# Attention times V with V stationary in four column tiles, the sums of E as one more row, outputs repacked and normalized through DRAM scratch

## The chip, the cores and the metric

One core of a Trainium2 chip runs the whole program. The metric is the device time of one execution in microseconds (us). Several executions are taken of each kernel, and the kernel before is run again on the same chip beside every kernel that is compared with it. A ratio is the mean time of one kernel's fast runs over the mean of the other's fast runs of the same rounds, so it is not quite the ratio of the medians quoted here. For a single core, a run is called slow if it lies over 1.5% above the fastest of its kernel.

Engine names in the profile: PE is TensorE's matmul, PEld its weight load, DVE is VectorE, ACT is ScalarE, POOL is GpSimd, SP is the engine that issues DMAs. "Tile" below means 128 rows (tokens) of the sequence, "block" two tiles.

## The reference

Two rounds of a sliding-window attention layer and an MLP, on 2048 tokens of width 512, with 32 heads of 16:

```python
def _A_ref(x, wqkv, wo):
    H = 32; Dh = D // H; W = 256
    q, k, v = ...                                 # x @ wqkv, split into heads
    scores = einsum("bhqd,bhkd->bhqk", q, k) * Dh ** -0.5
    mask = (i - j >= 0) & (i - j < W)
    p = softmax(where(mask, scores, -1e9))
    o = einsum("bhqk,bhkd->bhqd", p, v)
    return merge_heads(o) @ wo
def _B_ref(x, w1, b1, w2, b2):                    # F = 1792
    return gelu(x @ w1 + b1) @ w2 + b2
x = x + _A_ref(_layernorm(x), ...); x = x + _B_ref(_layernorm(x), ...)     # twice
```

The window is two tiles wide, so a tile of queries needs the keys of three tiles. The kernels skip the maximum in the softmax, compute E = exp(scores) with keys on partitions and queries along the free dimension, and divide by the sum at the end.

## The kernel before

The kernel is written as a list of nodes, each with an engine, a duration in ns and a priority. A planner simulates the engines with these durations, picks for each engine the ready node of lowest priority number, and the order that comes out is fixed: on the chip every engine executes its list strictly in order and waits on semaphores.

```python
class _Plan:
    LAT = {"pe": 230.0, "act": 110.0, "dve": 110.0, "pool": 150.0, "sp": 100.0}
    def add(self, eng, fn, dur, reads=(), writes=(), prio=0.0, ...): ...
    def run(self):
        ...                                       # cut: list scheduling in planned time
                if e == "sp":
                    efree[e] = t + 60.0           # an issue of a DMA holds the queue 60 ns
                else:
                    efree[e] = end
        return order
```

PV of one tile and one parity of heads takes E as the stationary operand: for each of four heads and three key tiles a 128x128 piece of E is loaded and 17 columns of V move (16 of the head, one of ones, which gives the sum). The result has tokens on partitions, so 1/sum is one number per partition and head, and O has to be transposed afterwards for the output projection.

```python
def pvm(e, B):
    for r in range(RG):                           # RG = 4 heads
        h = c * HC + 2 * r + par
        for k in range(kmin, t + 1):              # up to 3 key tiles
            x = e.matmul(ps[:, B[g][0], r * VW : (r + 1) * VW],            # VW = 17
                E[:, eslot(tau - t + k, v), r, blk * P : (blk + 1) * P],   # stationary
                Va[:, (tau - t + k) % VR, h, :], start=(k == kmin), stop=(k == t))
add("pe", pvm, ...)
add("dve", reciprocal(R[:, rs, :], <column 16 of each head>), 120, ...)
add("dve", tensor_tensor(out=Otm[...], in0=<O in PSUM>, in1=R[...], op=ALU.mult), ...)
...
def outproj(tau, prio):
    # four transposes of Otm, one copy to OT, then four matmuls with Wo
def mlp(J, ...):                                  # one MLP job for every four tiles
```

The layernorm's last step, `xn = (X - mean) * rstd`, is a VectorE `tensor_scalar`, planned at 330 ns.

The softmax here doesn't subtract the row's maximum and nothing guards it: scores larger than these inputs give would overflow.

## Time and profile before

| | before |
|---|---|
| median of 3 runs | 695.31 us (692.96 to 698.25) |
| TensorE busy | 581.8 us (84%) |
| ScalarE / VectorE / GpSimd busy | 65% / 61% / 31% |
| mean granted TensorE clock | 0.906 |
| first exponential starts | 50.3 us |

The profile page of the kernel before, its first lines and the chain of work that ended last (the path of waits followed back from the end):

```profile
span 694.4 us, 14552 instructions
PE 581.8 (84%) x5984; PEld 298.2 (43%) x5984; DVE 423.9 (61%) x1249; ACT 451.9 (65%) x640; POOL 217.4 (31%) x381
...
PE 56%; DVE 27%; ACT 9%; issue 5%; POOL 2%; POOLq 0%; DVEq 0%
PE ps L504 44%; DVE E L600 6%; PE ps L625 5%; ACT E L593 5%; PE ps L582 5%; DVE KT L540 5%; DVE X L513 4%; ACT E L596 3%; DVE stat L470 3%; DVE xn L480 2%; DVE Va L553 2%; DVE Otm L639 2%; PE ps L488 2%; DVE R L636 1%; DVE QT L532 1%
```

TensorE leads the chain; L504 is the helper that issues all projection and MLP matmuls, L625 is PV. No DMA stands in the chain. The groups of instructions by line that the change touches (busy us, mean ns of one, then idle time of the engine before them):

```profile
L625 PE MATMUL ps<-Va,E 128*128 128x17 bf16 x2880 | 112.4, 173 | 32.1 <-DVE Otm L639 7.7
L639 DVE TENSOR_TENSOR Otm<-ps,R 128x64 bf16<-128x64 f32 x256 | 56.3, 220 | 5.6
L636 DVE RECIPROCAL R<-ps 128x4 f32<-128x4 f32 x256 | 44.6, 174 | 14.6 <-PE ps L625 13.6
```

The timeline of TensorE shows a score group of four row tiles and a PV group of twelve matmuls (start us, length us). Twelve PV matmuls take 0.46 us, 38 ns each:

```profile
606.07 0.34 PE L582 MATMUL ps<-QT,KT 32*128 32x384 bf16 x4 [0.52 <-ACT E L593]
606.35 0.46 PE L625 MATMUL ps<-Va,E 128*128 128x17 bf16 x12
```

Busy time by stretches of the middle (length, then busy us and instructions of PE, PEld, DVE, ACT, POOL; granted clock; DMA share; GB/s):

```profile
300.00:400.00 100.00, 89.08 (x858) 45.68 (x856) 61.39 (x184) 69.54 (x109) 23.05 (x41) 0.91 0.01 1
400.00:500.00 100.00, 90.72 (x925) 45.57 (x925) 65.14 (x186) 69.47 (x95) 35.84 (x58) 0.93 0.01 4
```

In the middle TensorE is busy 90% of the time, and the DMA engines do next to nothing (share 0.01).

### The profile page before, as it was taken

What the parts mean: (1) busy time and instruction counts of PE and PEld (TensorE: products, weight loads), DVE (VectorE), ACT (ScalarE), POOL (GpSimd) and SP (SyncE); (2) the same over time, 40 slices, a digit from 0 to 9 for tenths busy, and PEclk for the clock granted to TensorE, in tenths of its full rate; (3) what the DMA queues carried; (4) which work ended last, traced back from release to release, by engine and by line L of the source; (5) the groups of instructions that cost most, each with busy time, mean ns of one, the idle gap of its engine ahead of it and who ended that gap; (6) DMA issues with size and microseconds to landing.
All of it is one profiled execution on the core that took longest, in us unless ns stands there. A gap on an engine that the chain in (4) does not pass through costs nothing.

```text
span 694.4 us, 14552 instructions
## 1 busy us (share of the span) xinstructions
PE 581.8 (84%) x5984; PEld 298.2 (43%) x5984; DVE 423.9 (61%) x1249; ACT 451.9 (65%) x640; POOL 217.4 (31%) x381
## 2 busy tenths in 40 slices
PE   0277888898889898899978898898989898799878
PEld 0143445444444444544444444444344444344433
DVE  0399788837683767838485677837486574625511
ACT  0008798788388836786187955779488964877340
POOL 2235455315341424400152243414243232410000
PEclk9998687999999888997989999899999998688989
DMA  9400000000000000000000000000000000000000
GB/s 312 142 1 1 1 3 1 2 1 1 1 2 2 2 1 1 2 1 1 1 1 2 1 1 1 2 2 2 23 9 2 1 8 24 1 2 9 24 1 30
DMA packets 10740, 10.89 MB, mean 16 GB/s; under 512 B 2226, under 2 KB 10163, under 8 KB 10675
## 3 DMA queue, kind: packets, MB, share of 16 engines
q1 hardware_dynamic: 10674, 9.97, 4.4%
q8 instruction: 47, 0.77, 0.5%
q14 instruction: 19, 0.15, 0.1%
HBM read 7.87 MB, written 2.10 MB: 14 GB/s over the span
## 4 chain that ended last, share of the span: by engine, by line
PE 56%; DVE 27%; ACT 9%; issue 5%; POOL 2%; POOLq 0%; DVEq 0%
PE ps L504 44%; DVE E L600 6%; PE ps L625 5%; ACT E L593 5%; PE ps L582 5%; DVE KT L540 5%; DVE X L513 4%; ACT E L596 3%; DVE stat L470 3%; DVE xn L480 2%; DVE Va L553 2%; DVE Otm L639 2%; PE ps L488 2%; DVE R L636 1%; DVE QT L532 1%
## 5 line engine op out<-in xcount | busy, mean ns | idle before, releaser
L593 ACT ACTIVATE E<-ps 128x768 bf16<-128x768 f32 (+2 forms) x256 | 198.8, 777 | 197.0 <-PE ps L582 195.2
L605 POOL TENSOR_SCALAR_AFFINE_SELECT E<-E 128x512 bf16<-128x512 bf16 x224 | 161.6, 722 | 264.2 <-ACT E L596 263.8
L596 ACT ACTIVATE E<-ps 128x768 bf16<-128x768 f32 (+2 forms) x256 | 199.0, 777 | 0.0
L625 PE MATMUL ps<-Va,E 128*128 128x17 bf16 x2880 | 112.4, 173 | 32.1 <-DVE Otm L639 7.7
L600 DVE TENSOR_TENSOR E<-E,mask 128x512 bf16<-128x512 bf16 x256 | 123.4, 484 | 20.6 <-ACT E L596 19.7
L625 PEld LDWEIGHTS ps<-Va,E 128*128 128x128 bf16 x2880 | 95.0, 98 | 86.5 <-issue 30.3
L504 PE MATMUL ps<-W_sb,gT 128*128 128x512 bf16 x448 | 113.8, 396 | 0.0
L582 PE MATMUL ps<-QT,KT 32*128 32x384 bf16 (+2 forms) x1024 | 92.3, 350 | 20.3 <-ACT E L593 19.1
L504 PE MATMUL ps<-xnTB,W_sb 128*128 128x512 bf16 x448 | 104.2, 388 | 0.5 <-DVE xnTB L493 0.5
L513 DVE TENSOR_TENSOR X<-X,ps 128x512 bf16<-128x512 bf16 x64 | 44.0, 687 | 91.4 <-PE ps L504 91.1
L684 ACT ACTIVATE gT<-ps,b1T 128x512 bf16<-128x512 f32 x112 | 76.4, 687 | 28.4 <-PE ps L504 28.0
L504 PE MATMUL ps<-xnTA,Wqkv_sb 128*128 128x256 bf16 x512 | 84.3, 311 | 7.4 <-DVE KT L540 4.9
L474 POOL TENSOR_SCALAR veps<-statmv 128x1 f32<-128x1 f32 x64 | 14.9, 233 | 174.4 <-DVE statmv L472 174.0
L504 PEld LDWEIGHTS ps<-xnTB,W_sb 128*128 128x128 bf16 x448 | 42.9, 99 | 50.0 <-issue 3.5
L488 PE MATMUL ps<-ident,xn 128*128 128x128 bf16 x256 | 27.7, 239 | 43.4 <-DVE xn L480 37.4
L504 PEld LDWEIGHTS ps<-W_sb,gT 128*128 128x128 bf16 x448 | 40.9, 100 | 53.4 <-issue 15.4
L504 PEld LDWEIGHTS ps<-xnTA,Wqkv_sb 128*128 128x128 bf16 x512 | 49.2, 108 | 26.7 <-DVE KT L540 7.1
L639 DVE TENSOR_TENSOR Otm<-ps,R 128x64 bf16<-128x64 f32 x256 | 56.3, 220 | 5.6
L663 DVE COPY OT<-ps 128x512 bf16<-128x512 bf16 x32 | 13.4, 419 | 73.9 <-PE ps L658 73.3
L582 PEld LDWEIGHTS ps<-QT,KT 32*128 32x128 bf16 x1024 | 26.3, 93 | 74.4 <-ACT E L593 46.7
L636 DVE RECIPROCAL R<-ps 128x4 f32<-128x4 f32 x256 | 44.6, 174 | 14.6 <-PE ps L625 13.6
L540 DVE TENSOR_SCALAR KT<-ps,parmask 128x512 bf16<-128x512 f32 x64 | 46.3, 738 | 4.4 <-PE ps L504 4.1
(34 smaller groups left out, 374.7 us busy)
## 6 DMA issues: line engine op xcount, KB each, us to landing
W_sb<-in_B_w_dram SPq DMA_DIRECT2D x2, 1792.0 KB, 14.7
out_dram<-X SPq DMA_DIRECT2D x16, 128.0 KB, 1.7
Wqkv_sb<-in_A_wqkv_dram SPq DMA_DIRECT2D x3, 512.0 KB, 5.6
X<-in_A_x_dram SPq DMA_DIRECT2D x1, 1024.0 KB, 11.0
X<-in_A_x_dram SPq DMA_DIRECT2D x2, 256.0 KB, 3.5
X<-in_A_x_dram SPq DMA_DIRECT2D x1, 512.0 KB, 7.9
Wo_sb<-in_A_wo_dram SPq DMA_DIRECT2D x1, 512.0 KB, 8.6
b1raw<-in_B_b_dram SPq DMA_DIRECT2D x1, 3.5 KB, 15.5
```

What stands on the lines that cost most here:

```text
L504: r = e.matmul(ps[:, B[g][0], cols], lhsT, rhs, start=st, stop=sp)
L513: add("dve", lambda e, B: e.tensor_tensor(out=X[:, t, :], in0=X[:, t, :], in1=ps[:, B[g][0], :], op=ALU.add), d_psum(512), reads=["X%d" % ...
L540: kn = (add("dve", lambda e, B, g=g, i=i, par=par: e.tensor_scalar(out=KT[:, kb, par, 2 * i : 2 * i + 2, :], in0=ps[:, B[g][0], :].rearran ...
L582: x = e.matmul(ps[:, bk[r], 0:N], KT[rows, kb, par, c, kc0 : kc0 + P], QT[rows, c, t * P : t * P + N], start=True, stop=True)
L593: a = add("act", lambda e, B, gT3=gT3, es=es: e.activation(E[:, es, 0:2, 0:N], ps[:, B[gT3][0] : B[gT3][0] + 2, 0:N], AF.Exp, scale=SCALE) ...
L596: a2 = add("act", lambda e, B, gS1=gS1, es=es: e.activation(E[:, es, 2:4, 0:N], ps[:, B[gS1][0] : B[gS1][0] + 2, 0:N], AF.Exp, scale=SCALE ...
L600: add("dve", lambda e, B, es=es: e.tensor_tensor(out=E[:, es, :, 0:P], in0=E[:, es, :, 0:P], in1=mask01[:, None, :].to_broadcast([P, RG, P ...
L605: add("pool", lambda e, B, es=es: e.affine_select(E[:, es, :, 2 * P : 3 * P], E[:, es, :, 2 * P : 3 * P], [[0, RG], [-1, P]], ALU.is_ge, 0 ...
L625: x = e.matmul(ps[:, B[g][0], r * VW : (r + 1) * VW], E[:, eslot(tau - t + k, v), r, blk * P : (blk + 1) * P], Va[:, (tau - t + k) % VR, h ...
L636: add("dve", lambda e, B: e.reciprocal(R[:, rs, :], ps[:, B[g][0], 0 : RG * VW].rearrange("p (b d) -> p b d", d=VW)[:, :, Dh]), 120, reads ...
L639: add("dve", lambda e, B: e.tensor_tensor(out=Otm[:, s, c * P : (c + 1) * P].rearrange("p (r a d) -> p r a d", a=2, d=Dh)[:, :, par, :], i ...
L684: gelu_last[0] = add("act", lambda e, B, g=g, fc=fc: e.activation(gT[:, fc, :], ps[:, B[g][0], :], AF.Gelu_apprx_tanh, bias=b1T[:, fc : fc ...
```

## The change

The intent: let TensorE spend less on PV. V (17 columns) becomes the stationary operand, and E, which is wide, moves. Four heads go to four column tiles of the array, so their outputs lie 32 partitions apart in one PSUM bank, with the sum of E as row 16 of each. O arrives transposed, which saves the transposes, but its rows lie in the wrong partitions and the sums lie on other partitions than O. So the bank is copied to SBUF (`OD`), written to DRAM scratch, read back repacked (`On`); the sums are read as 64 rows (`Dc`), inverted, written out again and read back broadcast over 16 partitions (`Rn`); GpSimd multiplies.

```diff
+ for pi, (k, q_lo, q_hi) in enumerate(parts):          # k in (-1, 0, -2, 1)
+     for r in range(RG):
+         x = e.matmul(ps[32 * r : 32 * r + VW, B[g][0], par * 256 + q_lo * P : par * 256 + (q_hi + 1) * P],
+                      Va[:, (2 * b + k) % VR, h, :],                            # stationary, 17 columns
+                      E[:, es, r, (q_lo - k) * P : (q_hi + 1 - k) * P], ...)    # moving, 128 or 256
+ evac(OD[:, s] <- ps)                                    # VectorE, or ScalarE if idle
+ dma(scr[bs, c].rearrange("j r n -> r j n") <- OD[:, s].rearrange("p a q -> p (a q)"))   # scr: (2, 4, 32, 4, 512)
+ dma(On[:, c, :] <- scr[bs, c, 0:Dh].rearrange("j r (a q) -> (j r a) q", a=2))
  ...                                                     # once per block of two tiles:
+ dma(Dc[:, bs, :] <- scr[bs, :, Dh].rearrange("c r (k n) -> c (r k) n", n=P))
+ add("dve", reciprocal(Rc[:, bs, :], Dc[:, bs, :]), 960, ...)
+ dma(scr_r[bs] <- Rc[:, bs, :])
+ for c in range(DC):
+     dma(Rn[:, c, :] <- scr_r[bs, c] broadcast to 16 partitions)
+     add("pool", tensor_tensor(OT[:, bs, c, :], On[:, c, :], Rn[:, c, :], mult), 500, ...)
```

Much else moves with it. The planner may now place some work on either of two engines, its formulas for matmuls, VectorE and ScalarE are changed a little, and all DMAs of the chain are planned at 2.0 us:

```diff
- def dma(fn, writes, reads=(), dur=3000.0, prio=0.0):
+ def dma(fn, writes, reads=(), dur=2000.0, prio=0.0):
      add("dve", tensor_scalar(out=xn[:, s, :], in0=X[:, t, :], ...), 330, ...
+         alt=(("pool", tensor_scalar(out=xn[:, s, :], in0=X[:, t, :], ...), 700, POOL_H),))
+ # masks of E: VectorE or GpSimd; OD copies: VectorE or ScalarE
+ JOBS = [(0, 2), (2, 2), (4, 4), (8, 4), (12, 4), (16, 4), (20, 4), (24, 4), (28, 2), (30, 2)]
- qkv(0, -40)
- qkv(1, -30)
+ lnq(0, -60); kv(0, -50); lnq(1, -40)                    # K and V of block 1 later
  ...                                                     # cut: visits go by blocks, K in one VectorE pass
```

## The prediction

> **What bounds the kernel now.** The page: TensorE busy 84% (582 of 694 us), ScalarE 65%, VectorE 61%, GpSimd 31%; granted clock 0.906. In the middle (300 to 500 us, table by windows) TensorE is busy 90%, ScalarE 70%, VectorE 63%. The chain that ended last is 56% TensorE, 27% VectorE, 9% ScalarE. So TensorE bounds, but not alone: exponentials pace the score groups, and small VectorE work gates TensorE through its two general PSUM banks. From spacings in the timeline (216 ns per 512-column matmul, 12 PV matmuls in 0.46 us) I estimate 503 us of TensorE work at full clock, 555 at the granted one.
>
> **Removed.** PV is 2880 matmuls of 17 columns, each with a 128-column weight load: 112 us busy, 38 ns each in the timeline. Also gone: 256 reciprocals (44.6 us) and 256 multiplies into Otm (56.3 us) on VectorE, 128 transposes of O (13.9 us), their 32 copies (13.4 us).
>
> **Added.** 1920 PV matmuls, V stationary (17 columns), 256 or 128 columns of E moving, four at a time. If four column tiles run side by side, one head parity of a two-tile block streams 768 columns (320 ns) plus some 40 ns per step: 0.45 to 0.6 us instead of 0.92; in all 55 to 70 us instead of 112. [...]this trace shows only row tiles together (four 384-column score matmuls in 0.21 to 0.3 us). Further 64 evacuations of 128x512 f32 (about 0.69 us each, estimated from the V and Q copies), on VectorE or idle ScalarE; 16 reciprocals of 64x128 (about 1 us); 64 GpSimd multiplies; 14 DMAs per block of two tiles. An output DMA takes 1.7 us, so the chain of four from the last evacuation to Rn takes 8 to 12 us, hidden by the next block's work, except in the last one.
>
> **Moved.** MLP jobs begin and end with two tiles instead of four, so the last MLP (27 us of TensorE, nothing behind it) halves: -14 us. First exp is at 50.3 us; K and V of block 1 no longer stand before it: -5 us. VectorE's wait for b1raw until 27 us stays. Masks, xn and evacuations go to whichever engine is free.
>
> **Sum.** TensorE: 503 - 111 + 60 - 8 = about 445 us at full clock, 480 to 490 at the granted clock. VectorE 424 -> 365 us. ScalarE 450 -> 465 us. TensorE and ScalarE are then nearly balanced, each 85 to 90% busy in the middle; each waits for the other, so not all of the gain arrives. On the critical path: PV, about 35 us of the chain (5%), halved; R and Otm, about 21 us, gone; tail and head about 20; better mixing of MLP and attention 10 to 20. That gives 695 - 85 = about 608 us, range 572 to 645.
>
> Faster by over 2%: 0.92; within 2%: 0.06; slower: 0.02.
>
> **What would show it.** PV busy 50 to 75 us, four PV matmuls starting within tens of ns of each other; TensorE busy 490 to 510 us; VectorE 350 to 380 us; ScalarE over 75% of the span; first exp near 45 us; last exp to end about 30 us; short waits of TensorE on OT.
>
> **What would make it wrong.** Column tiles that don't overlap (PV 170 us or more: no gain or slower); DMA chains longer than planned, so that in-order TensorE waits at the output projection of every block (2 to 4 us x 16); GpSimd's multiplies and masks contending with VectorE; a lower clock when TensorE idles more.

The sum: about 445 us of TensorE at full clock, 695 - 85 = about 608 us in all. The 320 ns for 768 columns can be worked out from the trace's 216 ns for 512 columns (324 ns), the 40 ns per step from its 38 ns for one PV matmul; both are estimates. The reciprocal's "about 1 us" is near the 960 ns of the changed plan; the trace after gives 945 ns.

## The result, and the profile after

The changed kernel takes 787.44 us (784.18 to 788.19, 4 runs) against 696.58 us (692.96 to 698.25) of the kernel before in the same rounds: ratio 1.130, 95% interval 1.124 to 1.136. It is 13% slower, and correct. The page after, the lines that answer to those of before:

```profile
span 786.3 us, 12367 instructions
PE 544.9 (69%) x4943; PEld 256.8 (33%) x5008; DVE 356.8 (45%) x659; ACT 471.1 (60%) x697; POOL 377.6 (48%) x519
...
DMA 33%; PE 23%; POOL 16%; ACT 14%; DVE 8%; issue 3%; SPq 2%; POOLq 0%; DVEq 0%
PE ps L547 17%; DMA scr_o<-OD 15%; ACT E L650 12%; POOL xn L524 8%; DMA Rn<-scr_r 7%; DMA Dc<-scr_o 5%; POOL OT L736 4%; DMA scr_r<-Rc 3%; POOL rstd L517 2%; PE ps L637 2%; DMA b1raw<-in_B_b_dram 2%; DVE Rc L728 2%; PE ps L693 2%; DVE X L556 2%; PE ps L531 1%
```

TensorE and VectorE have less to do, as intended, and TensorE is idle 786.3 - 544.9 = 241 us instead of 113. The chain is led by DMAs (33%), and GpSimd's xn (L524) is in it with 8%. The groups:

```profile
L524 POOL TENSOR_SCALAR xn<-X,statmv,rstd 128x512 bf16<-128x512 bf16 x48 | 100.8, 2099 | 10.1 <-PE ps L531 8.3
L693 PE MATMUL ps<-E,Va 128*17 128x128 bf16 (+1 forms) x1920 | 60.6, 274 | 16.2 <-DVE E L655 6.9
L547 PE MATMUL ps<-Wo_sb,OT 128*128 128x512 bf16 x120 | 41.2, 486 | 61.7 <-POOL OT L736 61.4
```

PV itself is as hoped: 60.6 us busy instead of 112.4, and in the timeline sixteen PV matmuls (four column tiles, four steps) take 0.51 us, where the kernel before needed twice 0.46 us for the same work:

```profile
401.74 0.51 PE L693 MATMUL ps<-E,Va 128*17 128x256 bf16 x16
```

But TensorE waits 61 us for OT, in 14 waits of up to 8.3 us:

```profile
PE ps L547 <- POOL OT L736: 61.4, 14, 8.3
```

VectorE executes in order too. It stands still for 96 us in front of its 16 reciprocals, until Dc lands, and all its later work waits with it:

```profile
L728 DVE RECIPROCAL Rc<-Dc 64x128 f32<-64x128 f32 x16 | 15.1, 945 | 96.1 <-DMA Dc<-scr_o 96.1
```

GpSimd needs 2.1 us for an xn that the plan had at 0.7 us. The chain from the last copy of OD of a block to its output projection, in order of time (start us, length us):

```profile
423.29 5.85 DMA scr_o<-OD
...
429.52 2.49 DMA Dc<-scr_o
432.01 0.02 issue
432.03 0.96 DVE Rc L728
...
433.05 1.79 DMA scr_r<-Rc
434.84 0.02 issue
434.86 2.55 DMA Rn<-scr_r
...
440.37 1.04 PE ps L547 x2
```

It takes 440.37 - 423.29 = 17.1 us, of which 14.1 us pass until the first Rn has landed (434.86 + 2.55 = 437.41). Over the 16 blocks, counted in the trace, the medians are 17.7 us, and 14.3 us until the first Rn and 16.2 us until the fourth. By the durations in the plan (2.0 + 2.0 + 0.96 + 2.0 + 2.0, and four multiplies at 0.5) it would have taken 11 us. TensorE had the output projection planned into the middle of an MLP job and stands still for 7.79 us before it (the same place in TensorE's timeline):

```profile
423.77 8.81 PE L547 MATMUL ps<-xnTB,W_sb 128*128 128x512 bf16 x40
440.37 1.04 PE L547 MATMUL ps<-Wo_sb,OT 128*128 128x512 bf16 x2 [7.79 <-POOL OT L736]
```

The DMA queue's own waits (in total us, times, longest) show what the slow write does to the queue. SP executes in order too, and the read of On behind each write waits for it:

```profile
SPq L711 <- DMA scr_o<-OD: 263.9, 50, 5.9
```

The stretches of the middle again:

```profile
300.00:400.00 100.00, 70.95 (x660) 32.61 (x668) 46.68 (x87) 60.92 (x98) 44.69 (x62) 0.85 0.21 57
400.00:500.00 100.00, 75.42 (x651) 33.39 (x657) 51.71 (x93) 64.73 (x90) 54.49 (x73) 0.87 0.18 50
```

No engine is over 76% busy, which points to waits and not to the work of one engine. The mean granted clock fell from 0.906 to 0.839. In the stretch from 432 to 441 us, with the 7.79 us gap, the table by windows gives a granted clock of 0.70 (the number before the last two), and from 436 to 445 us, with matmuls again from 440 us on, 0.50:

```profile
432.00:441.00 9.00, 1.21 (x5) 0.37 (x4) 0.95 (x1) 1.13 (x2) 2.77 (x4) 0.70 0.22 62
```

Before the gap, at a granted clock of 1.00, 40 matmuls of 128x512 took 8.81 us, 0.22 us each; after it, at 0.51 (441.6 to 445.8 us), four of the same size took 1.91 us, 0.48 us each:

```profile
442.48 1.91 PE L547 MATMUL ps<-Wo_sb,OT 128*128 128x512 bf16 x4
```

So part of such a wait is paid a second time, in slower matmuls; e4 below sizes that part. That the gap itself lowers the clock is the author's reading: the trace shows the one after the other. Nor would long gaps be all that moves the clock: in the kernel before, TensorE is never idle for more than 3.2 us once it has begun, and the mean clock is still 0.906, not 1. What lowers it there is not shown.

### The profile page after: what moved, and what is told of

Read it like the earlier page. It is cut to its first block, busy times and chain, and to the rows that moved or that the text cites. A ratio compares the mean times of both kernels' runs of the same rounds, so it can differ in the third digit from the quotient of the medians.

```text
span 786.3 us, 12367 instructions
## 1 busy us (share of the span) xinstructions
PE 544.9 (69%) x4943; PEld 256.8 (33%) x5008; DVE 356.8 (45%) x659; ACT 471.1 (60%) x697; POOL 377.6 (48%) x519
## 4 chain that ended last, share of the span: by engine, by line
DMA 33%; PE 23%; POOL 16%; ACT 14%; DVE 8%; issue 3%; SPq 2%; POOLq 0%; DVEq 0%
PE ps L547 17%; DMA scr_o<-OD 15%; ACT E L650 12%; POOL xn L524 8%; DMA Rn<-scr_r 7%; DMA Dc<-scr_o 5%; POOL OT L736 4%; DMA scr_r<-Rc 3%; POOL rstd L517 2%; PE ps L637 2%; DMA b1raw<-in_B_b_dram 2%; DVE Rc L728 2%; PE ps L693 2%; DVE X L556 2%; PE ps L531 1%
## 5 line engine op out<-in xcount | busy, mean ns | idle before, releaser
L650 ACT ACTIVATE E<-ps 128x768 bf16<-128x768 f32 (+2 forms) x512 | 354.0, 782 | 175.3 <-PE ps L637 174.0
L778 ACT ACTIVATE gT<-ps,b1T 128x512 bf16<-128x512 f32 (+1 forms) x140 | 81.9, 603 | 99.2 <-PE ps L547 98.8
L655 DVE TENSOR_TENSOR E<-E,mask 128x512 bf16<-128x512 bf16 x218 | 107.9, 497 | 68.6 <-ACT E L650 67.2
L547 PE MATMUL ps<-xnTB,W_sb 128*128 128x512 bf16 (+1 forms) x554 | 112.5, 356 | 13.6 <-DVE Va L498 12.5
L736 POOL TENSOR_TENSOR OT<-On,Rn 128x256 bf16<-128x256 f32 x64 | 45.7, 743 | 152.7 <-DMA Rn<-scr_r 152.6
L547 PE MATMUL ps<-W_sb,gT 128*128 128x512 bf16 x414 | 115.9, 398 | 3.7 <-issue 3.5
L524 POOL TENSOR_SCALAR xn<-X,statmv,rstd 128x512 bf16<-128x512 bf16 x48 | 100.8, 2099 | 10.1 <-PE ps L531 8.3
L547 PE MATMUL ps<-xnTA,Wqkv_sb 128*128 128x256 bf16 x512 | 83.3, 316 | 17.9 <-DVE OD L498 6.7
L547 PE MATMUL ps<-Wo_sb,OT 128*128 128x512 bf16 x120 | 41.2, 486 | 61.7 <-POOL OT L736 61.4
L547 PEld LDWEIGHTS ps<-xnTB,W_sb 128*128 128x128 bf16 x560 | 56.1, 103 | 63.5 <-DVE Va L498 14.3
L693 PE MATMUL ps<-E,Va 128*17 128x128 bf16 (+1 forms) x1920 | 60.6, 274 | 16.2 <-DVE E L655 6.9
L547 PEld LDWEIGHTS ps<-xnTA,Wqkv_sb 128*128 128x128 bf16 x512 | 52.0, 111 | 42.9 <-DVE OD L498 7.2
L547 PEld LDWEIGHTS ps<-W_sb,gT 128*128 128x128 bf16 x448 | 37.8, 100 | 51.9 <-issue 24.6
L693 PEld LDWEIGHTS ps<-E,Va 128*17 128x17 bf16 x1920 | 41.4, 99 | 39.1 <-issue 20.5
L531 PEld LDWEIGHTS ps<-ident,xn 128*128 128x128 bf16 x256 | 18.2, 110 | 85.2 <-POOL xn L524 41.5
```

What stands on the lines that cost most here:

```text
L524: alt=(("pool", lambda e, B: e.tensor_scalar(out=xn[:, s, :], in0=X[:, t, :], scalar1=statmv[:, k, 0:1], scalar2=rstd[:, k : k + 1], op0=A ...
L531: r = e.transpose(psb[:, B[g][0], c * P : (c + 1) * P], xn[:, s, c * P : (c + 1) * P], ident[:])
L547: r = e.matmul(ps[:, B[g][0], cols], lhsT, rhs, start=st, stop=sp)
L650: a = (add("act", lambda e, B, g=g, gi=gi: e.activation(E[:, es, 2 * gi : 2 * gi + 2, 0:N], ps[:, B[g][0] : B[g][0] + 2, 0:N], AF.Exp, sca ...
L655: add("dve", lambda e, B: e.tensor_tensor(out=E[:, es, :, 0:P], in0=E[:, es, :, 0:P], in1=mask01[:, None, 0, :].to_broadcast([P, RG, P]), ...
L693: x = e.matmul(ps[32 * r : 32 * r + VW, B[g][0], par * 256 + q_lo * P : par * 256 + (q_hi + 1) * P], Va[:, (2 * b + k) % VR, h, :], E[:, e ...
```

## The experiments

Three theories. **Theory 1:** the DMA chain is longer than planned, above all because the write of OD is slow, and the in-order engines wait for it. **Theory 2:** GpSimd's xn, three times as long as planned, is the loss. **Theory 3:** the new order, or the column-tiled PV, is itself worse. A first set keeps the planned order of the changed kernel instruction for instruction and alters only what is executed at one place of it ("same planned order"); a second set plans anew. Each new plan is another order, and how far the time moves between equally good plans was not measured, so a few microseconds between such runs (e5, e6, e7, e9, e11, e12) mean nothing. The experiments ran on three chips, on which the kernel before took 695.2, 695.9 and 696.1 us.

### e1: xn on VectorE, same planned order

```diff
  for i in order:
      nd = PL.nodes[i]
+     if nd["eng"] == "pool" and nd["writes"] and nd["writes"][0][:2] == "xn":
+         nd["eng"], nd["fn"] = nd["alts"][0][:2]        # VectorE
```

> The changed kernel in its planned order, instruction for instruction; only the 48 normalizations (xn) that it put on GpSimd at 2.1 us each run on VectorE instead (0.4 to 0.8 us). Theory 1 (the DMA chain from OD to Rn is longer than planned, and TensorE, in order, waits at the output projection): little, 787 -> 760 to 780 us, DMA stays above 28% of the chain of waits. Theory 2 (GpSimd's xn, three times as long as planned, is the main loss): 787 -> 720 us or less. Theory 3 (the new order itself, or the column tiled PV, is the loss): within 1% of 787.

Measured: 754.70 us (752.13 to 756.31, 4 runs), ratio 1.085 to the kernel before (695.23). xn on VectorE takes 0.41 us (median); in the changed kernel the 16 that stayed there took 0.79 us. The time falls by 33 us, less than theory 2 asked for and more than theory 1 alone gave it. DMA is 36% of the chain. So xn is a cause, and, as e2 will show, the smaller one.

### e2: the write of OD in four parts, same planned order

```diff
- scr[bs, c].rearrange("j r n -> r j n") <- OD[:, s]                      # 4 x 32 x 512
+ for r in range(RG):  scr[bs, c, :, r, :] <- OD[32 * r : 32 * r + 32, s] # 32 x 512 each
```

> The changed kernel in its planned order; only each write of OD to the scratch (256 KB, landing 5.9 us after issue) is issued as four writes of 32 partitions each, to the same addresses. If the write is slow because its scratch side has 4 as its outermost dimension, [...]the last of the four lands some 3.5 to 4.2 us after the first issue (four issues of 0.5 us and 2 us), and by theory 1 the time falls by 15 to 40 us (the OD link of the chain was 15% of 786 us). If 256 KB in runs of 2 KB simply takes that long, landing stays near 6 us or more, and the time stays or grows with the issue time. Theories 2 and 3: within 1% of 787.

Measured: 709.37 us (707.79 to 710.84, 4 runs), ratio 1.021. The same bytes go to the same addresses, and the kernel is 78 us faster, about twice the 15 to 40 us expected. In the timeline of the DMA queue the read of On, which waits for the write, is issued 5.81 us after the write in the changed kernel, and 3.08 us after the first of the four here (medians of all 64: 5.85 and 3.20 us). First the changed kernel, then e2:

```profile
403.18 0.56 SPq L708 DMA_DIRECT2D scr_o<-OD  x1
408.99 0.33 SPq L711 DMA_DIRECT2D On<-scr_o  x1
```

```profile
300.36 1.71 SPq L711 DMA_DIRECT2D scr_o<-OD  x4
303.44 0.34 SPq L713 DMA_DIRECT2D On<-scr_o  x1
```

Why the landing time goes with the shape is not shown; no view of the profile shows single DMA engines. What the trace of the changed kernel shows is that the single write leaves most of the capacity of the 16 DMA engines unused: from 340 to 344 us, inside one write (issued at 338.56, its read of On at 344.34 us) and with no other DMA issued meanwhile, their mean busy share is 0.25 (the number before the last), and inside two others (331 to 335 and 363 to 367 us) 0.20 and 0.22:

```profile
340.00:344.00 4.00, 3.95 (x21) 1.93 (x20) 1.18 (x1) 3.69 (x7) 0.64 (x1) 1.00 0.25 66
```

That is the full time of 3 to 4 engines (an estimate: 0.20 to 0.25 of 16). The shapes differ in the outermost dimension of the scratch side: it is 4 in the single write (4 x 32 x 512) and 32 in each of the four (32 x 512); e10 tries 2. The read of Dc also has 4 outermost on the scratch side; it moves only 32 KB in 2.45 us, and no run tried it otherwise.

### e3: both, same planned order

> Both edits of e1 and e2 together, same order. Theory 1 and 2 both at work: the gains add to about 787 -> 700 to 740 us. If one hides the other, the gain is that of the larger alone or more than the sum.

Measured: 676.82 us (675.38 to 678.41, 4 runs), ratio 0.974: faster than the kernel before, and below the 700 to 740 us expected, because e2 gained more than expected. The gains of e1 (33 us) and e2 (78 us) add to the 111 us measured here, so neither hides the other. The chain now takes 11.8 us until the first Rn and 13.8 us until the fourth (medians of 16 blocks), and TensorE still waits 40 us for OT.

### e4: no chain, same planned order (wrong result)

```diff
+ memset(Rn, 1.0); memset(On, 0.01)                        # once, at the start
  for i in order:
+     if nd["writes"] and nd["writes"][0][:2] in ("S0", "S1", "On", "Dc", "Rc", "SR", "Rn"):
+         continue                                         # no scratch DMA, no reciprocal
```

> Wrong result on purpose. As e1 (xn on VectorE, same planned order), and all DMAs through the scratch and the 16 reciprocals are left out; OT is computed by the same 64 GpSimd multiplies from constants, so that the output projection waits for no DMA. Everything else, PV and the OD evacuations too, stays. Theory 1: the chain is the main loss, so the time falls below that of the kernel before, to 600 to 650 us, TensorE idle for OT near 0. Theory 3 (order or PV itself): stays above 690 us.

Measured: 627.24 us (625.35 to 627.99, 4 runs), ratio 0.902; results wrong. TensorE waits 9 us for OT, and its mean clock is 0.929.

```profile
PE ps L547 <- POOL OT L736: 9.2, 7, 1.9
```

With the same order for all the rest, the changed kernel without chain and with xn on VectorE is 10% faster than the kernel before. Theory 3 falls: neither the order nor the column tiles are worse by themselves.

Against e1 (same order, same matmuls, same xn) the span falls by 127 us, and the two traces say where. TensorE's wait for OT falls by 51 us (59.9 to 9.2). Its waits for what VectorE makes (Va, X, OD, KT and masked E, lines L547 and L693) fall by 47 us (53 to 6): in e1 VectorE stands 97 us for Dc, and here there is no Dc. And its busy time falls by 34 us (547.4 to 513.3), as the clock rises from 0.859 to 0.929: the same matmuls run faster. So the chain cost TensorE in three ways, and the wait for OT is less than half of it. The chain that ended last is TensorE and ScalarE now:

```profile
PE 41%; ACT 34%; DVE 11%; POOL 7%; DMA 4%; issue 1%; SPq 1%; DVEq 0%
```

### e10: the write of OD in two parts, same planned order (one look)

```diff
- for r in range(RG):       scr[bs, c, :, r, :] <- OD[32 * r : 32 * r + 32, s]
+ for r in range(0, RG, 2): scr[bs, c, :, r : r + 2, :].rearrange("j r n -> r j n") <- OD[32 * r : 32 * r + 64, s]   # 2 x 32 x 512
```

> One look, as e3 and in the same planned order, but OD written in two DMAs of 64 partitions (scratch side outermost dimension 2) in place of four of 32 partitions (outermost 32) or one of 128 (outermost 4). [...]the last lands later than the single write did: 8 us or more after the first issue. If many smaller DMAs are faster for being many, it lies between: 4 to 5.5 us.

Measured: 877.83 us (one run, state unknown), correct. xn is on VectorE, as in e3. The read of On is issued 8.20 us after the first of the two writes (median of 64: 8.66 us):

```profile
304.19 1.13 SPq L711 DMA_DIRECT2D scr_o<-OD  x2
312.39 0.32 SPq L713 DMA_DIRECT2D On<-scr_o  x1
```

One write of 128 partitions 5.8 us, two of 64 8.2 us, four of 32 3.1 us: the number of writes alone does not order these times, the outermost dimension of the scratch side (4, 2, 32) does. The 8 us or more of the expectation was the estimate for the case that this dimension decides; why two writes take longer than one is not shown either.

### e8: one more link in the chain, same planned order as e3

```diff
  dma(scr_r[bs] <- Rc[:, bs, :])
+ dma(scr_x[bs] <- scr_r[bs])                              # 32 KB, scratch to scratch
- dma(Rn[:, c, :] <- scr_r[bs, c] broadcast)
+ dma(Rn[:, c, :] <- scr_x[bs, c] broadcast)
```

> As e3, same planned order, with one more link in the chain of each block: the reciprocals are copied from scratch to scratch (32 KB, some 2 us) before Rn is read. 16 blocks. Theory 1 (the chain's end stands on the critical path of nearly every block): 677 -> 700 to 712 us. If the chain is mostly hidden by now: under 685 us.

Measured: two fast runs at 718.38 and 726.93 us, two called slow at 730.39 and 730.58; ratio of the fast ones 1.041 (one of the seven runs of the kernel before beside it is called slow too). The profile shows 1.95 us for one added copy, some 31 us for 16 blocks. The fast runs are 42 and 50 us above e3, more than the 23 to 35 us expected. So the chain's end stands on the critical path of nearly every block, and a microsecond there costs more than one. The profiled run (a slow one) has TensorE waiting 70 us for OT (40 in e3) and a clock of 0.864 (0.909 in e3); how the surplus divides between clock, queue and other waits stays open.

### e9: only the planner's numbers

```diff
- xn on GpSimd 700, OD write 2000, Dc 2000, Rn 2000, OT multiply 500, an issue on SP 60
+ xn on GpSimd 2100, OD write 5900, Dc 2450, Rn 2600, OT multiply 730, an issue on SP 430
```

> The changed kernel with all its operations and engine choices (OD in one write, GpSimd may still take xn); only numbers in the planner are replaced by measured ones: xn on GpSimd 2.1 us instead of 0.7, OD write 5.9 us instead of 2.0, Dc 2.45, Rn 2.6, 430 ns for each issue instead of 60, OT multiply 0.73 instead of 0.5. If the loss is the mismatch of plan and chip (in-order engines waiting where the plan saw none), it falls from 787 to 640 to 690 us without any faster operation. If the slow operations themselves are the loss, it stays above 740 us.

Measured: 700.98 us (696.81 to 706.64, 4 runs), ratio 1.008. No operation was rewritten. The planner still puts 41 of the 64 xn on GpSimd at 2.1 us (48 before) and keeps the slow write; the order and the choices of engine now know the true durations. That recovers 86 of the 91 us lost. It is above the 640 to 690 us expected: a 5.9 us write can be planned around, but not for nothing. TensorE waits 29 us for OT (61 before the new plan).

### e6: both repairs, planned with measured durations

```diff
+ OD in four parts (1800 each), xn on VectorE alone
+ Dc 2450, Rn 2600, OT multiply 730, an issue on SP 430
```

> As e3 (OD written in four parts, xn on VectorE), but planned anew with the durations that the trace shows: 1.8 us a part, 2.45 us for Dc, 2.6 us for Rn, 430 ns for each issue on the queue, 730 ns for the OT multiply. If the remaining loss (e3 677 against e4 627) comes from a chain longer than the plan believed, a plan that knows it puts other work in the gap: 640 to 660 us, TensorE waiting for OT under 15 us (40 in e3). If the chain's length itself can't be hidden, it stays within 1% of 677.

Measured: 629.77 us (628.61 to 630.82, 4 runs), ratio 0.907. This is below the 640 to 660 us expected. TensorE waits 7 us for OT, although the chain is no shorter than in e3 (12.5 us until the first Rn): it is hidden now.

```profile
PE ps L544 <- POOL OT L734: 7.0, 8, 2.1
```

The real chain, planned with real numbers, costs hardly more than no chain at all in the old order (e4, 627 us). The chain that ended last:

```profile
PE 40%; ACT 26%; DVE 12%; DMA 12%; POOL 5%; SPq 3%; issue 2%; DVEq 0%; ACTq 0%; POOLq 0%
```

### e5: the old PV in the new frame

E stationary, reciprocal, Otm and transposes as in the kernel before; all the rest (blocks, MLP jobs, K in one pass, choices of engine) as in the changed kernel, xn on VectorE, planned anew.

```diff
- pv(c): V stationary, OD, scratch, Dc, Rc, Rn, GpSimd multiply
+ pvgroup(v, j): E stationary, R, Otm; outproj with four transposes and one copy     # from the kernel before
```

> The changed kernel's planner, MLP jobs, q/k/v order and engine choices, but PV, 1/sum, Otm and the transposes of O as in the kernel before (E stationary, no scratch), xn on VectorE; planned anew. It undoes the PV swap and nothing else of the change. If the swap itself is worth its TensorE time once its chain is out of the way, this is slower than e4's 627 us by 30 to 60 us, so 655 to 690. If the gain seen in e3 and e4 comes from the new planning alone, it runs at 640 us or less.

Measured: 691.84 us (690.19 to 696.67, 4 runs), ratio 0.997: the same as the kernel before. TensorE is busy 580.8 us here and 513.4 us in e6, and e6 is 62 us faster. So the swap is worth about its TensorE time, and the rest of the change alone (with xn on VectorE) is worth nothing measurable. Part of these 67 us of busy time may be clock: 0.911 here, 0.934 in e6.

### e7: a version without scratch

V is padded to 32 columns, `[V | 0]` for even heads and `[0 | V]` for odd ones, so both heads of a pair add into the same 32 rows and O lies as the output projection wants it. A second pass of E over a block of ones gives the sums, already broadcast.

```diff
+ matmul(ps[32 * r : 32 * r + 32, bank, 0:256],   Va[..., 32 columns], E[...])     # both parities into one group
+ matmul(ps[32 * r : 32 * r + 32, bank, 256:512], ones2[:, par, :],    E[...])
+ evac(OD); reciprocal(Rd, OD[:, s, 1, :]) on VectorE; OT = OD[:, s, 0, :] * Rd on GpSimd
```

> A version without scratch: V stationary padded to 32 columns (zeros in the other head's half), so both heads of a pair add into the same 32 PSUM rows and O lands in the order that the output projection needs; the sums come from a second pass of E over a block of ones, already broadcast to 16 rows; VectorE takes 1/sum of 128x256 (planned at 1.9 us each), GpSimd multiplies. PV matmuls double (3840). TensorE busy some 50 us above e4's 513, VectorE some 460 us. Expected 640 to 680 us; below e3's 677 if the chain is what costs e3 its last 50 us.

Measured: 644.81 us (644.61 to 645.51, 4 runs), ratio 0.929, correct. TensorE is busy 542.7 us, the reciprocals of 128x256 take 1743 ns each (112 us of VectorE). It beats the kernel before without any DMA chain; e6 beats it by 15 us. Its TensorE is busy 29 us longer than in e6 and its VectorE 70 us; which of them costs the 15 us was not tested, and its other durations were not measured anew.

### e11 and e12: both kernels with measured durations

e11 is the kernel before with measured durations in its planner; e12 is e6 with the same numbers for the loads, rstd and xn.

```diff
- loads 3000 (e11) or 2000 (e12) to 20000, b1raw 3000 or 2000, rstd 200, xn 330
+ loads 3500 to 27000, b1raw 28000, rstd 580, xn 410
+ e11 also: matmul N / 2.4 + 12, PV 38 a matmul, reciprocal 174, Otm 220, PSUM reads + 150, an issue on SP 430; a few more cut
```

> The kernel before, planned anew with measured durations (the first loads 3.5 to 28 us, rstd 0.58 us, xn 0.41, PV 38 ns a matmul, reciprocal 174 ns, and the matmul, VectorE and ScalarE formulas of the changed kernel). A control: if measured durations alone bring what e6 brought, 640 us or less. If PV as it is keeps TensorE the bound, 670 to 692 us, of which some 10 to 15 us come from the start alone (VectorE no longer waits for b1raw until 28 us).

> As e6, and the same measured durations of loads, rstd and xn as in e11: VectorE no longer waits for b1raw, so the first transposes start near 10 us instead of 29. Expected 605 to 620 us; first exp near 30 us. Against e11 it tells what the swap is worth when both are planned with measured numbers: 50 to 75 us if the swap's TensorE saving arrives.

Measured: e11 683.53 us (682.30 to 683.92, 4 runs), ratio 0.982; e12 611.98 us (606.54 to 615.34, 4 runs), ratio 0.881, interval 0.877 to 0.886. VectorE no longer waits for b1raw, and the first exponential starts at 27.7 us (e11) and 23.1 us (e12). With honest plans on both sides the whole change (xn on VectorE) is worth 683.5 - 612.0 = 72 us. Not all of that need be saved work: the mean clock is 0.857 in e11 and 0.941 in e12, though TensorE in e11 is never idle for more than 3.2 us once it has begun. Why e11 has the lower clock is not shown. e12 is the fastest version made here, 12% below the kernel before.

| kernel | us | differs by |
|---|---|---|
| before | 696 | |
| after | 787 | |
| e1 | 755 | after, xn on VectorE |
| e2 | 709 | after, OD write in four parts |
| e3 | 677 | both |
| e4 (wrong result) | 627 | e1, no chain |
| e9 | 701 | after, measured durations in the plan |
| e6 | 630 | both repairs, measured durations |
| e12 | 612 | e6, loads measured too |
| e5 / e11 | 692 / 684 | old PV, new frame / before, measured durations |

## Why the prediction was wrong

It said 608 us, range 572 to 645, and 92% for faster; measured were 787 us.

- **Right: PV.** It said 55 to 70 us busy and 0.45 to 0.6 us for one parity of a block; measured 60.6 us and 0.51 us. Four column tiles do run side by side.
- **Right: VectorE.** 350 to 380 us said, 356.8 us measured. First exponential near 45 us said, 46.4 us measured.
- **Right as a ceiling: the gain.** The TensorE time that the swap saves does become run time when nothing else stands in the way: e4 at 627 us and e6 at 630 us lie inside the range.
- **Wrong, the main step: "the chain of four from the last evacuation to Rn takes 8 to 12 us, hidden by the next block's work, except in the last one."** From the write of OD to the first Rn it took 14.3 us (median of 16 blocks; 16.2 us to the fourth), and it was not hidden: TensorE waited 61 us for OT and VectorE 96 us for Dc. The size failed because it was taken from the 1.7 us of one output DMA, without looking at the shapes: the write of OD has 4 as outermost dimension on the scratch side and took 5.85 us (e2: 3.2 us in four parts; e10: 8.7 us in two; medians). The hiding failed because the order is fixed by a plan that had 2.0 us for each DMA (e9: with true numbers in the plan and the slow write kept, 86 of the 91 us come back). Of the two, the hiding is the deeper fault: in e3 the chain takes 11.8 us until the first Rn, inside the predicted 8 to 12, and TensorE still waits 40 us; in e6 it takes 12.5 us and TensorE waits 7. "DMA chains longer than planned, 2 to 4 us x 16" stood among the things that would make it wrong; the wait for OT alone came to that. "A lower clock when TensorE idles more" stood there too (TensorE idle 241 us instead of 113, clock 0.839 instead of 0.906); VectorE, which stands in order behind Dc, did not. By e1 against e4, waits for VectorE and slower matmuls cost 47 and 34 us of TensorE's time, beside 51 us for OT.
- **Wrong, the second step: "Masks, xn and evacuations go to whichever engine is free."** It was counted as a gain of balance, without a price. xn takes 2.1 us on GpSimd and 0.41 us on VectorE, and 48 of 64 went there; e1 prices this at 33 us.
- **Wrong as a consequence: the engines' balance.** ScalarE "over 75% of the span" came to 60%, and TensorE's busy time to 545 us instead of 490 to 510, at a granted clock of 0.839. In e4, with clock 0.929, it is 513 us.
- **Wrong: the end.** From the last exponential to the end 30 us were said; it was about 53 us (733.4 to 786.3 us). The last block has the whole chain ahead of its output projection, as was foreseen, but from its last write of OD (740.1 us) to that projection (758.5 us) it took 18.4 us.
- **Not at work:** columns that don't overlap. **At work, its share of the loss not tested:** GpSimd beside VectorE. Of the 16 xn left on VectorE (median 0.79 us; 0.41 us in e1), the ten that began within 0.13 us after an xn on GpSimd, which runs 2.1 us, took 0.79 to 0.80 us; the one with no GpSimd instruction beside it took 0.40 us.

## What to carry to other kernels

When a kernel is ordered by a plan and executed in order, every duration in the plan is part of the kernel: a new kind of operation (a DMA of a new shape, an old operation on another engine) is to be measured once and its number put into the plan before the change is judged. For a DMA through scratch, look at the outermost dimension of the scratch side before anything else (256 KB took 5.85 us with 4, 8.66 us in two writes with 2, 3.20 us in four with 32), and read its landing time by shape, not from another DMA of similar size. Taking a suspected wait away with the planned order kept, even with a wrong result, tells in one run whether the idea or its plumbing is at fault.

## Durations measured here, by shape

- A write of 256 KB to DRAM, from the first issue to the read that waits for it (medians): 5.85 us with outermost dimension 4, 8.66 us in two writes with 2, 3.20 us in four writes with 32.
- tensor_scalar with two per-partition scalars on bf16, 128x512: 2.09 us on GpSimd and 0.41 us on VectorE (medians, after and e1), 5 times as long, while an affine_select of the same size takes 0.73 us on GpSimd.
- Reciprocal on VectorE: 64x128 f32 takes 945 ns, 128x256 takes 1743 ns (e7), some 6 ns for each further element of a partition (an estimate from these two).
- Four column tiles with 17 columns: sixteen matmuls of 128 or 256 columns in 0.51 us, where the same work with E stationary took 0.92 us.
